# Six late token blocks take their first MLP product by Strassen's scheme

## The chip, the cores and the metric

The kernel runs on one core of a Trainium2 chip. The metric is the device time of one execution, in microseconds (us). A core has TensorE (PE, with PEld for its weight loads), VectorE (DVE), ScalarE (ACT), GpSimd (POOL) and SyncE (SP), which issues most transfers. TensorE writes its products into the eight banks of PSUM, and DVE and ACT take them from there.

## The reference

The input is 4 sequences of 3008 tokens with 256 features. A Fourier transform along the sequence, a complex 256x256 product with soft shrinkage, and the inverse transform give `x` again; then a two-layer MLP works on all 12032 tokens:

```python
X = np.fft.rfft(x, axis=1)
Yr = Xr @ w_r - Xi @ w_i + b_r;  Yi = Xr @ w_i + Xi @ w_r + b_i
Yr, Yi = shrink(Yr, 0.01), shrink(Yi, 0.01)
x = np.fft.irfft(Yr + 1j * Yi, n=3008, axis=1).reshape(12032, 256)
h = x @ w_in                          # 256 -> 2048
out = (h / (1 + exp(-h))) @ w_out     # 2048 -> 256
```

## The kernel before, in words

**Precision.** The large products run in the type fp32r on operands split into a high part and a low part, so one product is three matmuls: high by high, low by high and high by low. A "matmul" below is one instruction with a 128x128 weight; its cost goes with the columns that it streams.

**The MLP.** Tokens are taken in 24 blocks of 512 (the last, block 23, has 256). A block passes through 16 ticks, one for each 128 of the 2048 hidden features. In a tick `mlp1` makes six matmuls of 512 columns (L523: two halves of the 256 features, three terms each) into one PSUM bank `h`, of which there are two, and ACT writes Silu of it to `g` (L530). One tick later `split_g` makes the high part `gh` on ACT (L539) and the low part `gl` on DVE (L540). Two ticks after `mlp1`, `mlp2` multiplies them with `w_out` into four accumulator banks `acc`: for each 128 tokens one matmul of 512 columns (L562) and one of 256 (L566). After a block's last tick the four banks are added up and stored (`o`, ACT L582, DVE L583).

**The filler work.** The transforms of the four sequences are small steps that a table hangs on ticks, between a tick's `mlp1` and its `mlp2`: `at` puts a step on a tick, `put` on the next free one. `u3_step` (lines `s2_3`, `mix3`, `i1`) is one of twelve units of the middle transform of a sequence; for sequence 3 the units start at tick 190 and are 4.8 ticks apart. The last step, `i2`, multiplies stored rows with a table (L466) and splits the result into the high and the low part `xt` of a block's input (ACT L482, DVE L483); it comes in two halves and an end piece, `i2_ends` (L492 to L503, which hands leftover columns on to the next block as `rest`), each on a tick of its own, some 7, 5 and 3 ticks ahead of the block. Each engine works through its instructions in the order in which the program lists them, and waits on semaphores of the other engines.

The loop that lists the work of a tick:

```python
for t in range(len(ticks) + 2):
    split_g(*ticks[t - 1])
    ...
    mlp1(*ticks[t])
    for fn, args in fill.pop(t, []):
        fn(*args)
    flush(1 if t < 12 else 4)
    mlp2(*ticks[t - 2])
```

## Time and profile before

| | |
|---|---|
| runs | 1366.64, 1367.81, 1369.87 us; median 1367.81 |
| profiled execution | span 1366.0 us from first to last instruction; the page lists no time around it, and the median run is 1.8 us longer, the fastest 0.6 |
| PE | 1352.8 us busy, 99% |
| ACT, DVE | 727.9 us (53%), 686.1 us (50%) |
| chain that ended last | PE 96%, DMA 3%, ACT 1% |

The page gives each engine's busy time, then the span in slices, the transfers, the chain of work that ended last and the costliest groups. TensorE is busy for nearly the whole span, so the other views are read for what its instructions cost and for how closely ACT and DVE follow it.

### The profile page before, as it was taken

How to read it: one execution, taken by the hardware profiler on the slowest of the kernel's cores; microseconds unless marked ns; L12 is line 12 of the kernel's file. 1: busy time of each engine (PE TensorE's matmuls, PEld its weight loads, DVE VectorE, ACT ScalarE, POOL GpSimd, SP SyncE). 2: the span in 40 equal slices, each digit the busy share in tenths (PEclk: the TensorE clock that was granted, in tenths of full speed). 3: DMA queues.
4: the chain of work that ended last, by engine and by line, in shares of the span. 5: the costliest groups of instructions: out<-in, count | busy, mean ns of one | idle time of the engine just before them, and what ended most of it. 6: DMA issues, size and time to landing. Idle time of an engine off the chain costs nothing.

```text
span 1366.0 us, 20164 instructions
## 1 busy us (share of the span) xinstructions
PE 1352.8 (99%) x7589; PEld 1163.0 (85%) x7589; DVE 686.1 (50%) x1200; ACT 727.9 (53%) x1418; POOL 126.0 (9%) x192
## 2 busy tenths in 40 slices
...
GB/s 269 257 217 192 121 52 107 63 97 36 129 112 86 107 73 93 116 91 110 40 99 69 55 71 70 58 90 24 62 34 10 28 40 23 5 28 39 4 13 24
DMA packets 72753, 109.74 MB, mean 80 GB/s; under 512 B 8400, under 2 KB 54224, under 8 KB 72656
## 3 DMA queue, kind: packets, MB, share of 16 engines
...
q14 instruction: 37, 0.30, 0.1%
...
## 4 chain that ended last, share of the span: by engine, by line
PE 96%; DMA 3%; ACT 1%; issue 0%; DVE 0%; SPq 0%; ACTq 0%
PE h L523 38%; PE acc L562 25%; PE acc L566 13%; PE mix L376 6%; PE i L466 3%; PE s L351 2%; PE i L424 2%; PE mix L315 2%; PE s L254 1%; DMA scr<-i1o 1%; PE acc L557 1%; DMA scr<-s1o 1%; PE i2e L466 1%; PE i L421 1%; PE s L218 1%; PE s L294 1%
## 5 line engine op out<-in xcount | busy, mean ns | idle before, releaser
L523 PE MATMUL h<-xt,win 128*128 128x512 f32 (+1 forms) x2304 | 584.8, 389 | 0.0
L562 PE MATMUL acc<-wout,gh 128*128 128x512 f32 x1472 | 539.3, 400 | 0.0
L530 ACT ACTIVATE g<-h 128x512 f32<-128x512 f32 (+1 forms) x385 | 226.2, 588 | 511.2 <-PE h L523 509.2
L523 PEld LDWEIGHTS h<-xt,win 128*128 128x128 f32 x2304 | 400.9, 188 | 82.0 <-DVE xt L483 0.4
L540 DVE TENSOR_TENSOR gl<-g,gh 128x512 fp32r<-128x512 f32 (+1 forms) x385 | 264.6, 689 | 349.9 <-ACT gh L539 348.2
L566 PE MATMUL acc<-wout,gl 128*128 128x256 f32 x1472 | 411.9, 280 | 0.0
L562 PEld LDWEIGHTS acc<-wout,gh 128*128 128x128 f32 x1472 | 276.8, 188 | 58.6 <-issue 0.3
L566 PEld LDWEIGHTS acc<-wout,gl 128*128 128x128 f32 x1472 | 278.0, 189 | 9.7 <-issue 0.2
L539 ACT CAST gh<-g 128x512 fp32r<-128x512 f32 (+1 forms) x385 | 235.2, 611 | 5.2
L383 POOL TENSOR_TENSOR q<-q,bias 128x256 f32<-128x256 f32 x36 | 26.4, 734 | 592.8 <-ACT q L382 592.8
L483 DVE TENSOR_TENSOR xt<-i,xt 128x376 fp32r<-128x376 f32 (+2 forms) x48 | 28.1, 586 | 77.1 <-ACT xt L482 73.1
L256 DVE TENSOR_TENSOR s1o<-s,s1o 48x512 f32<-48x512 f32 x64 | 41.0, 678 | 48.2 <-ACT s1o L255 46.5
L466 PEld LDWEIGHTS i<-c_sb,gin 96*128 96x128 f32 x420 | 54.4, 192 | 9.6 <-issue 3.8
L396 DVE TENSOR_TENSOR y<-q,mix 64x256 f32<-64x256 f32 x144 | 60.3, 419 | 2.1
L466 PE MATMUL i<-c_sb,gin 96*128 96x94 f32 x420 | 53.7, 272 | 4.0 <-DMA gin<-scr 4.0
L245 DVE TENSOR_TENSOR sx<-x_sb,sx 47x1024 fp32r<-47x1024 f32 x32 | 40.7, 1271 | 22.3 <-ACT sx L244 21.4
L361 DVE TENSOR_TENSOR xs<-s,xs 128x256 f32<-128x256 f32 x36 | 15.3, 424 | 70.9 <-ACT xs L360 70.9
L184 POOL DMA_DIRECT2D x_sb<-in_x_dram x64 | 32.8, 514 | 142.4 <-ACT sx L244 125.4
L583 DVE TENSOR_TENSOR o<-acc,o 128x256 f32<-128x256 f32 x92 | 33.0, 417 | 24.4 <-ACT o L582 24.4
L351 PEld LDWEIGHTS s<-t,a 128*128 128x128 f32 x288 | 37.7, 191 | 3.0
L351 PE MATMUL s<-t,a 128*128 128x128 f32 x288 | 37.9, 274 | 0.0
L384 POOL TENSOR_TENSOR q<-q,bias 128x256 f32<-128x256 f32 x36 | 37.5, 1042 | 2.8
...
## 6 DMA issues: line engine op xcount, KB each, us to landing
...
```

The costliest lines, as they stand in the source:

```text
L245: nc.vector.tensor_sub(sx[64:64 + RR, :], t[64:64 + RR, :], sx[64:64 + RR, :])
L256: nc.vector.tensor_tensor(out=o[:, c], in0=p[:2 * NR, :], in1=o[:, c], op=ALU.add)
L351: nc.tensor.matmul(out=pv[:, e, :, r, :], lhsT=a[:, r, e * 128:(e + 1) * 128], rhs=t2[:, r * 128:(r + 1) * 128], start=True, stop=True,)
L376: nc.tensor.matmul(out=out, lhsT=x_[:, e, c, :], rhs=m[:, e, :], start=(n == 0), stop=(n == 5))
L396: nc.vector.tensor_tensor(out=y[64 * i:64 * i + 64, r, :], in0=q[rows, i, :], in1=pv[rows, i, :], op=op,)
L466: nc.tensor.matmul(out=p[:, o:o + m], lhsT=g_t[b, j // 4][:, q:q + 128], rhs=c4_sb[:, p0:p0 + m], start=True, stop=True,)
L523: nc.tensor.matmul(out=p[:, :n], lhsT=w[:, e, f * 128:(f + 1) * 128], rhs=v[:, e, :n], start=(m == 0), stop=(m == 5),)
L530: nc.scalar.activation(out=g[:, q], in_=p[:, q], func=ACTF.Silu)
L539: nc.scalar.copy(gh[:, q], g[:, q])
L540: nc.vector.tensor_sub(gl[:, q], g[:, q], gh[:, q])
L562: nc.tensor.matmul(out=a, lhsT=gh[:, q], rhs=wout[:, f].rearrange("p a c -> p (a c)"), start=begins, stop=False,)
L566: nc.tensor.matmul(out=a[:, D:2 * D], lhsT=gl[:, q], rhs=wout[:, f, 0, :], start=False, stop=ends,)
```

## The change

For blocks 17 to 22 the first product is made differently. Two ticks are taken together: their 256 hidden features by 512 tokens are a matrix product of 2x2 parts (two halves of the features in, of the hidden features and of the tokens), which Strassen's scheme, in Winograd's form, makes with seven products of parts instead of eight. Each is three matmuls of 256 columns, so a pair of ticks has 21 matmuls of 256 columns instead of 12 of 512.

Sums of parts of `w_in` are made once, on DVE and ACT, in eight steps after the last transform step (`fast_weights`). Sums of parts of a block's input (`fast_moving`) need the input in full precision, which `i2` now copies to `xf` on ACT as well (L491, L503, L513 of the changed kernel). In the even tick of a pair `fast_one` makes four products into both `h` banks, px and py; ACT copies the first to `u`, DVE adds the second to it (`u`) and the other two to that (`g[3]`). In the odd tick `fast_two` adds the other three products into the same banks, and Silu and the splitting follow there. `mlp2` of such a block comes three ticks after, not two. The six blocks' `i2` stands six ticks earlier than before, and the units of sequence 3 are 4.2 ticks apart, not 4.8. Buffers of the transforms move to a pool `tf`, which is released after the last transform step; the new buffers are then taken from its space (`tl`).

```diff
+FAST = range(17, 23)
...
     sb = ctx.enter_context(tc.tile_pool(name="sb", bufs=2))
+    tf = tc.alloc_tile_pool(name="tf", bufs=1)
...
         nc.scalar.copy(h[:, e, q], p[:, q])
         nc.vector.tensor_sub(l[:, e, q], p[:, q], h[:, e, q])
+        if i in FAST:
+            if e == 0:
+                xf[i] = tl.tile([128, 2, BLK], F32, tag="xf", bufs=1, name="xf")
+            nc.scalar.copy(xf[i][:, e, q], p[:, q])
...
             nc.scalar.copy(h[:, :, q], t)
             nc.vector.tensor_sub(l[:, :, q], t, h[:, :, q])
+            if i in FAST:
+                nc.scalar.copy(xf[i][:, :, q], t)
...
             nc.scalar.copy(h[:, :, q], p[:, :, 0:m])
             nc.vector.tensor_sub(l[:, :, q], p[:, :, 0:m], h[:, :, q])
+            if i in FAST:
+                nc.scalar.copy(xf[i][:, :, q], p[:, :, 0:m])
             rest[i + 1] = sb.tile([128, 2, NP], F32, tag="rest", bufs=1, name="rest")[:, :, 0:NP - m]
             nc.scalar.copy(rest[i + 1], p[:, :, m:NP])
...
+    HB = BLK // 2
+    xf, th, tw, fast = {}, {}, {}, {}
+    def fast_weights(q):
+        k = slice(q * 256, (q + 1) * 256)
+        f32 = tl.tile([128, 2, 256], F32, tag="td", bufs=1, name="wf")
+        d = tl.tile([128, 4, 128], F32, tag="wd", bufs=2, name="wd")
+        nc.vector.tensor_tensor(out=f32, in0=win[0][:, :, k], in1=win[1][:, :, k], op=ALU.add)
+        a11, a21 = f32[:, 0, 0:128], f32[:, 0, 128:256]
+        a12, a22 = f32[:, 1, 0:128], f32[:, 1, 128:256]
+        nc.vector.tensor_tensor(out=d[:, 0, :], in0=a21, in1=a22, op=ALU.add)
+        nc.vector.tensor_sub(d[:, 1, :], d[:, 0, :], a11)
+        nc.vector.tensor_sub(d[:, 2, :], a11, a21)
+        nc.vector.tensor_sub(d[:, 3, :], a12, d[:, 1, :])
+        yield
+        hi = tl.tile([128, 4, 128], F32R, name=f"sw_h{q}")
+        lo = tl.tile([128, 4, 128], F32R, name=f"sw_l{q}")
+        nc.scalar.copy(hi, d)
+        yield
+        nc.vector.tensor_sub(lo, d, hi)
+        tw[q] = (hi, lo)
+    def fast_moving(i):
+        x32 = xf.pop(i)
+        d = tl.tile([128, 4, HB], F32, tag="td", bufs=1, name="td")
+        l0, r0, l1, r1 = x32[:, 0, 0:HB], x32[:, 0, HB:BLK], x32[:, 1, 0:HB], x32[:, 1, HB:BLK]
+        nc.vector.tensor_sub(d[:, 0, :], r0, l0)
+        nc.vector.tensor_sub(d[:, 2, :], r1, r0)
+        nc.vector.tensor_sub(d[:, 1, :], r1, d[:, 0, :])
+        nc.vector.tensor_sub(d[:, 3, :], l1, d[:, 1, :])
+        yield
+        hi = tl.tile([128, 4, HB], F32R, tag="th", bufs=2, name="th")
+        lo = tl.tile([128, 4, HB], F32R, tag="tl", bufs=2, name="tl")
+        nc.scalar.copy(hi, d)
+        yield
+        nc.vector.tensor_sub(lo, d, hi)
+        th[i] = (hi, lo)
+    def fast_product(p, i, q, a, b, begins):
+        w = [v[:, a, :] for v in tw[q]] if isinstance(a, int) else \
+            [v[:, a[0], q * 256 + a[1] * 128:q * 256 + a[1] * 128 + 128] for v in win]
+        m = [v[:, b, :] for v in th[i]] if isinstance(b, int) else \
+            [v[:, b[0], b[1] * HB:(b[1] + 1) * HB] for v in xt[i]]
+        for n, (j, k) in enumerate(((0, 0), (1, 0), (0, 1))):
+            nc.tensor.matmul(
+                out=p, lhsT=w[j], rhs=m[k], start=(begins and n == 0), stop=(n == 2), skip_group_check=True,
+            )
+    def fast_one(i, q):
+        px, py = [ps.tile([128, 512], F32, tag="h", bufs=2, name="h") for _ in range(2)]
+        fast_product(px[:, 0:HB], i, q, (0, 0), (0, 0), True)
+        fast_product(px[:, HB:BLK], i, q, 0, 0, False)
+        fast_product(py[:, 0:HB], i, q, 1, 1, True)
+        fast_product(py[:, HB:BLK], i, q, 2, 2, False)
+        u = tl.tile([128, HB], F32, tag="u", bufs=2, name="u")
+        g = tl.tile([128, 4, HB], F32, tag="gp", bufs=2, name="gp")
+        nc.scalar.copy(u, px[:, 0:HB])
+        nc.vector.tensor_tensor(out=u, in0=py[:, 0:HB], in1=u, op=ALU.add)
+        nc.vector.tensor_tensor(out=g[:, 3, :], in0=px[:, HB:BLK], in1=u, op=ALU.add)
+        nc.vector.tensor_tensor(out=g[:, 3, :], in0=py[:, HB:BLK], in1=g[:, 3, :], op=ALU.add)
+        fast[i, q] = (px, py, u, g)
+    def fast_two(i, q):
+        px, py, u, g = fast.pop((i, q))
+        fast_product(px[:, 0:HB], i, q, (1, 0), (1, 0), False)
+        fast_product(px[:, HB:BLK], i, q, 3, (1, 1), False)
+        fast_product(py[:, HB:BLK], i, q, (1, 1), 3, False)
+        nc.scalar.activation(out=g[:, 0, :], in_=px[:, 0:HB], func=ACTF.Silu)
+        nc.vector.tensor_tensor(out=g[:, 1, :], in0=px[:, HB:BLK], in1=u, op=ALU.add)
+        nc.vector.tensor_tensor(out=g[:, 2, :], in0=py[:, HB:BLK], in1=u, op=ALU.add)
+        nc.scalar.activation(out=g[:, 1, :], in_=g[:, 1, :], func=ACTF.Silu)
+        gs = [tuple(tl.tile([128, 2, HB], F32R, tag=f"g{k}", bufs=4, name=f"g{k}") for k in "hl") for _ in range(2)]
+        def low(r):
+            nc.vector.tensor_sub(gs[r][1], g[:, 2 * r:2 * r + 2, :], gs[r][0])
+        nc.scalar.copy(gs[0][0], g[:, 0:2, :])
+        low(0)
+        nc.scalar.activation(out=g[:, 2:4, :], in_=g[:, 2:4, :], func=ACTF.Silu)
+        nc.scalar.copy(gs[1][0], g[:, 2:4, :])
+        later.append(lambda: low(1))
+        for r in range(2):
+            gf[i, 2 * q + r] = tuple(v.rearrange("p a c -> p (a c)") for v in gs[r])
+    later = []
...
-            t = 16 * i - 9 if i > 1 else -1
+            t = (16 * i - 15 if i in FAST else 16 * i - 9) if i > 1 else -1
             if i > 1:
                 at(t, i2_load, i)
             put(t + 2, i2, i, 0)
             put(t + 4, i2, i, 1)
-            put(t + 6, i2_ends, i)
+            t = put(t + 6, i2_ends, i)
+            if i in FAST:
+                moving = fast_moving(i)
+                for k in range(3):
+                    at(t + 2 + k, next, moving, None)
...
-        for b, t0, dt in ((1, t + 11, 3.1), (2, 104, 4.3), (3, 190, 4.8)):
+        for b, t0, dt in ((1, t + 11, 3.1), (2, 104, 4.3), (3, 190, 4.2)):
...
+        def swap_pools():
+            nonlocal tl
+            tf.release()
+            tl = ctx.enter_context(tc.tile_pool(name="tl", bufs=1, reuse_waits="tile"))
+        at(last + 1, swap_pools)
+        for q in range(NFF // 2):
+            steps = fast_weights(q)
+            for k in range(3):
+                at(last + 2 + q + k, next, steps, None)
+        assert last + 11 < 16 * FAST[0]
+        done = 0
         for t in range(len(ticks) + 2):
-            if 0 <= t - 1 < len(ticks):
+            i, f = ticks[t] if t < len(ticks) else (LAST, None)
+            if 0 <= t - 1 < len(ticks) and ticks[t - 1][0] not in FAST:
                 split_g(*ticks[t - 1])
             while deferred:
                 deferred.pop(0)()
-            if t < len(ticks):
-                mlp1(*ticks[t])
+            if i in FAST:
+                (fast_two if f % 2 else fast_one)(i, f // 2)
+            elif t < len(ticks):
+                mlp1(i, f)
+            if f is None or i not in FAST or f % 2 == 0:
+                while later:
+                    later.pop(0)()
             for fn, args in fill.pop(t, []):
                 fn(*args)
             flush(1 if t < 12 else 4)
-            if t >= 2:
-                mlp2(*ticks[t - 2])
+            while done < t - (2 if i in FAST else 1):
+                mlp2(*ticks[done])
+                done += 1
```

What the program lists for TensorE in such blocks: before, the end of one tick's `mlp2` and the next tick's `mlp1` (names as in the text, `win_80` and `win_81` are the high and the low part of `w_in`, `xt_9448` and `xt_9449` those of a block; in brackets the semaphores that an instruction waits for).

```order
L562 MATMUL acc<-wout,gh 128x512
L566 MATMUL acc<-wout,gl 128x256
L523 MATMUL h<-xt_9448,win_80 128x512 [waits Activation_49]
L523 MATMUL h<-xt_9448,win_81 128x512
L523 MATMUL h<-xt_9449,win_80 128x512
L523 MATMUL h<-xt_9448,win_80 128x512
L523 MATMUL h<-xt_9448,win_81 128x512
L523 MATMUL h<-xt_9449,win_80 128x512
```

After, the same place with `fast_two` (`sw`: sums of parts of `w_in`; `th`, `tl`: sums of parts of the input).

```order
L665 MATMUL acc<-wout,gh 128x512
L669 MATMUL acc<-wout,gl 128x256
L602 MATMUL h<-xt_10451,win_83 128x256 [waits DVE_49,Activation_49]
L602 MATMUL h<-xt_10451,win_84 128x256
L602 MATMUL h<-xt_10452,win_83 128x256
L602 MATMUL h<-xt_10451,sw_h_10375 128x256
L602 MATMUL h<-xt_10451,sw_l_10376 128x256
L602 MATMUL h<-xt_10452,sw_h_10375 128x256
L602 MATMUL h<-th,win_83 128x256 [waits DVE_49]
L602 MATMUL h<-th,win_84 128x256
L602 MATMUL h<-tl,win_83 128x256
```

The wait on ACT alone, for the release of a bank, became a wait on ACT and DVE: for the copy `u` and for the DVE addition L617 that reads the other half of px; the wait of the last three is for L618.

What it lists for ScalarE where a half of `i2` stands, before:

```order
L530 ACTIVATE g<-h 128x512 [waits DVE_49,PE_49]
L539 CAST gh<-g 128x512 [waits Activation_49]
L530 ACTIVATE g<-h 128x512 [waits DVE_49,PE_49]
L482 CAST xt_10879<-i_10881 128x376 [waits PE_49]
L539 CAST gh<-g 128x512 [waits Activation_49]
L530 ACTIVATE g<-h 128x512 [waits DVE_49,PE_49]
```

And after, from the Silu of `fast_two` to the next pair's:

```order
L627 ACTIVATE gp<-h 128x256 [waits PE_49]
L630 ACTIVATE gp<-gp 128x256 [waits DVE_49]
L636 CAST gh<-gp 128x512 [waits Activation_49]
L638 ACTIVATE gp<-gp 128x512 [waits DVE_49]
L639 CAST gh<-gp 128x512 [waits Activation_49]
L486 CAST xt_11408<-i_11410 128x376 [waits PE_49]
L491 COPY xf<-i_11410 128x376 [waits DVE_49]
L615 COPY u<-h 128x256 [waits PE_49]
L627 ACTIVATE gp<-h 128x256 [waits PE_49]
```

The copy `u` of the next pair now stands behind the whole splitting of this one and, where there is an `i2`, behind two copies of it, the second of which waits for DVE (its L487, which reads the same bank).

What it lists for VectorE at the end of a block, before:

```order
L540 TENSOR_TENSOR gl<-g,gh 128x512 [waits DVE_49,PE_49,Activation_49] x3
L583 TENSOR_TENSOR o<-acc,o 128x256 [waits DMAHW4_49,DMAHW3_49,Activation_49]
L583 TENSOR_TENSOR o<-acc,o 128x256 [waits DMAHW6_49,DMAHW7_49,DMAHW0_49,Activation_49]
L583 TENSOR_TENSOR o<-acc,o 128x256 [waits DMAHW2_49,DMAHW1_49,Activation_49]
L583 TENSOR_TENSOR o<-acc,o 128x256 [waits DMAHW4_49,DMAHW5_49,DMAHW3_49,Activation_49]
L540 TENSOR_TENSOR gl<-g,gh 128x512 [waits DVE_49,Activation_49]
```

And after:

```order
L616 TENSOR_TENSOR u<-h,u 128x256 [waits PE_49,Activation_49]
L617 TENSOR_TENSOR gp<-h,u 128x256 [waits DVE_49]
L618 TENSOR_TENSOR gp<-h,gp 128x256 [waits DVE_49]
L634 TENSOR_TENSOR gl<-gp,gh 128x512
L686 TENSOR_TENSOR o<-acc,o 128x256 [waits DMAHW1_49,DMAHW7_49,DMAHW0_49,Activation_49]
L686 TENSOR_TENSOR o<-acc,o 128x256 [waits DMAHW4_49,DMAHW3_49,Activation_49]
L686 TENSOR_TENSOR o<-acc,o 128x256 [waits DMAHW6_49,DMAHW5_49,Activation_49]
L686 TENSOR_TENSOR o<-acc,o 128x256 [waits DMAHW1_49,DMAHW7_49,DMAHW0_49,Activation_49]
L628 TENSOR_TENSOR gp<-h,u 128x256 [waits Activation_49]
L629 TENSOR_TENSOR gp<-h,u 128x256 [waits PE_49]
```

The four additions of the finished block's output, which stood between two `gl`, now stand between the two halves of a pair: ahead of L628 and L629, whose results the Silu of that pair needs. L628 waits for ACT too (its Silu L627, which reads the other half of px).

## Rows read from the trace of the kernel before

**Rows 1.** The page, part 1: engine, busy time, share of the span, instructions.

```profile
PE 1352.8 (99%) x7589; PEld 1163.0 (85%) x7589; DVE 686.1 (50%) x1200; ACT 727.9 (53%) x1418; POOL 126.0 (9%) x192
```

**Rows 2.** Busy time by stretch, a block: PE, PEld, DVE, ACT, POOL, granted clock, DMA.

```profile
1062.00:1109.00 47.00, 47.00 (x247) 39.96 (x246) 14.23 (x26) 21.84 (x42) 0.00 (x0) 1.00 0.08 20
```

**Rows 3.** The chain that ended last, 1290 to 1312 us: start, length, what.

```profile
1290.48 1.39 PE h L523 x6
...
1309.99 1.39 PE h L523 x6
```

**Rows 4.** The same chain, 470 to 490 us.

```profile
474.22 0.86 PE i L466 x8
...
481.56 0.42 PE i2e L466 x4
...
484.80 2.15 PE mix L376 x18
```

**Rows 5.** Groups of TensorE, 1000 to 1340 us: busy us, mean ns, idle before.

```profile
L566 PE MATMUL acc<-wout,gl 128*128 128x256 f32 x468 | 131.0, 280 | 0.0
```

**Rows 6.** Groups of ScalarE, 1000 to 1340 us.

```profile
L539 ACT CAST gh<-g 128x512 fp32r<-128x512 f32 x115 | 71.4, 621 | 2.7
...
L582 ACT COPY o<-acc 128x256 f32<-128x256 f32 x31 | 10.0, 376 | 0.0
L482 ACT CAST xt<-i 128x470 fp32r<-128x470 f32 x6 | 3.3, 553 | 2.9 <-PE i L466 2.9
L482 ACT CAST xt<-i 128x376 fp32r<-128x376 f32 x6 | 2.8, 474 | 1.6 <-PE i L466 1.6
L530 ACT ACTIVATE g<-h 128x256 f32<-128x256 f32 x2 | 0.8, 385 | 2.2 <-PE h L523 2.2
...
L500 ACT CAST xt<-i2e 128x112 fp32r<-128x112 f32 x1 | 0.3, 256 | 0.0
```

**Rows 7.** Groups of VectorE, 1000 to 1340 us.

```profile
L540 DVE TENSOR_TENSOR gl<-g,gh 128x512 fp32r<-128x512 f32 x115 | 79.6, 692 | 181.1 <-ACT gh L539 180.9
L583 DVE TENSOR_TENSOR o<-acc,o 128x256 f32<-128x256 f32 x30 | 10.7, 417 | 13.5 <-ACT o L582 13.5
L483 DVE TENSOR_TENSOR xt<-i,xt 128x470 fp32r<-128x470 f32 x6 | 3.9, 648 | 14.9 <-ACT xt L482 14.9
L483 DVE TENSOR_TENSOR xt<-i,xt 128x376 fp32r<-128x376 f32 x6 | 3.3, 550 | 13.1 <-ACT xt L482 13.1
...
L501 DVE TENSOR_TENSOR xt<-i2e,xt 128x112 fp32r<-128x112 f32 x1 | 0.3, 268 | 0.0
```

**Rows 8.** Groups of the whole span: two shapes that stand nearest to added ones.

```profile
L245 DVE TENSOR_TENSOR sx<-x_sb,sx 47x1024 fp32r<-47x1024 f32 x32 | 40.7, 1271 | 22.3 <-ACT sx L244 21.4
...
L362 ACT CAST xh<-xs 128x256 fp32r<-128x256 f32 x36 | 14.6, 407 | 17.8 <-DVE xs L361 17.8
```

**Rows 9.** Timeline of one tick: start, length, engine, instruction, idle and releaser.

```profile
1299.61 0.62 PE L523 MATMUL h<-xt,win 128*128 128x512 f32 x2
...
1300.27 0.60 ACT L530 ACTIVATE g<-h 128x512 f32<-128x512 f32 x1 [1.54 <-PE h L523]
...
1300.89 0.62 ACT L539 CAST gh<-g 128x512 fp32r<-128x512 f32 x1
...
1301.55 0.69 DVE L540 TENSOR_TENSOR gl<-g,gh 128x512 fp32r<-128x512 f32 x1 [2.09 <-ACT gh L539]
```

**Rows 10.** Timeline, 705 to 710 us: two ScalarE instructions in a row.

```profile
707.02 0.55 ACT L482 CAST xt<-i 128x470 fp32r<-128x470 f32 x1 [0.49 <-PE i L466]
...
707.47 0.62 ACT L539 CAST gh<-g 128x512 fp32r<-128x512 f32 x1
```

**Rows 11.** Timeline, 1293 to 1300 us: the output of a block on VectorE.

```profile
1295.59 1.42 DVE L583 TENSOR_TENSOR o<-acc,o 128x256 f32<-128x256 f32 x4 [1.71 <-ACT o L582]
```

**Rows 12.** Timeline, 36 to 37.5 us: matmuls after a wait, then without one.

```profile
36.14 0.48 PE L315 MATMUL mix<-wr,xh 128*128 128x256 f32 x2
...
36.58 0.40 PE L315 MATMUL mix<-wi,xh 128*128 128x256 f32 x2
```

**Rows 13.** Waits from 110 us on: who waited for whom, us, times, longest.

```profile
ACT rest L503 <- DVE xt L501: 8.8, 22, 0.9
```

More of the change, by code (lines that the diff above doesn't have):

```diff
@@ L206, in s1 @@
             tag, bufs = ("s1o", 2) if 8 * b + g in (6, 7, 10, 11) else ("gin", 4)
-            o = sb.tile([128, 4 * D], F32, tag=tag, bufs=bufs, name="s1o")[:96, :]
+            o = (tf if tag == "s1o" else sb).tile([128, 4 * D], F32, tag=tag, bufs=bufs, name="s1o")[:96, :]
         for i in range(2):
@@ L212, in s1 @@
                 k, w, n = ("x", 768, 2) if g % 2 else ("g", 512, 3)
-                hl = [sb.tile([128, w], F32R, tag=k + q, bufs=n, name="sx")[:, :512] for q in "hl"]
+                hl = [(tf if k == "x" else sb).tile([128, w], F32R, tag=k + q, bufs=n, name="sx")[:, :512] for q in "hl"]
                 nc.vector.tensor_copy(out=hl[0], in_=h)
@@ L229, in s1_later @@
         if i == 0:
-            x_t[1, g, "o"] = sb.tile([128, 4 * D], F32, tag="s1o", bufs=2, name="s1o")[:96, :]
+            x_t[1, g, "o"] = tf.tile([128, 4 * D], F32, tag="s1o", bufs=2, name="s1o")[:96, :]
         o = x_t[1, g, "o"]
@@ L242, in stack_split @@
         t = x_t[b, q]
-        sx = sb.tile([128, 4 * D], F32R, tag="sx", bufs=1, name="sx")
+        sx = tf.tile([128, 4 * D], F32R, tag="sx", bufs=1, name="sx")
         nc.scalar.copy(sx[:64 + RR, :], t[:64 + RR, :])
@@ L249, in stack_product @@
         sx = x_t.pop((b, q))
-        o = sb.tile([128, 4 * D], F32, tag="s1o", bufs=2, name="s1o")[:2 * NR, :]
+        o = tf.tile([128, 4 * D], F32, tag="s1o", bufs=2, name="s1o")[:2 * NR, :]
         for i in range(2):
@@ L276, in t2_load @@
     def t2_load(b, u):
-        t2 = sb.tile([128, 256], F32, tag="t2", bufs=3, name="t2")
+        t2 = tf.tile([128, 256], F32, tag="t2", bufs=3, name="t2")
         nc.sync.dma_start(out=t2, in_=c2[:, u * 256:(u + 1) * 256])
@@ L283, in u_load @@
             t2_load(b, u)
-        a = sb.tile([128, 2, D], F32, tag="a", bufs=3, name="a")
+        a = tf.tile([128, 2, D], F32, tag="a", bufs=3, name="a")
         nc.sync.dma_start(out=a, in_=scr1[b][2 * u:2 * u + 2].rearrange("r p d -> p r d"))
@@ L297, in s2 @@
                 )
[L298 to L299 removed]
+        xh = tf.tile([128, 4, 192], F32R, tag="xh", bufs=2, name="xh")
+        xl = tf.tile([128, 4, 192], F32R, tag="xl", bufs=2, name="xl")
         nc.scalar.copy(xh[:, :, 64:192], pv)
@@ L329, in mix3_weights @@
     def mix3_weights():
-        t = sb.tile([128, 2, 2 * D], F32, tag="s1o", bufs=2, name="w32")
+        t = tf.tile([128, 2, 2 * D], F32, tag="s1o", bufs=2, name="w32")
         nc.sync.dma_start(out=t[:, :, 0:D], in_=w_r.rearrange("(e p) d -> p e d", p=128))
@@ L379, in mix3 @@
         p = bank("mix")
-        q = sb.tile([128, 2, D], F32, tag="q", bufs=1, name="q")
+        q = tf.tile([128, 2, D], F32, tag="q", bufs=1, name="q")
         product(p[:, 0:D], 2, wr)
@@ L406, in split_z @@
         y = u_t[b, u]
-        zh = sb.tile([128, 2, D], F32R, tag="zh", bufs=2, name="zh")
-        zl = sb.tile([128, 2, D], F32R, tag="zl", bufs=2, name="zl")
+        zh = tf.tile([128, 2, D], F32R, tag="zh", bufs=2, name="zh")
+        zl = tf.tile([128, 2, D], F32R, tag="zl", bufs=2, name="zl")
         nc.scalar.copy(zh, y)
```

50 lines of the change are left out of this document (25 added, 25 removed).

## The prediction

> **What bounds the kernel now.** I read the page's engine line first, then busy time by stretch, the chain, the groups by shape, and the timeline of one tick. PE is busy for 1352.8 of 1366.0 us [rows 1]. In the stretch of a block it is busy for all of 47.00 us at a granted clock of 1.00 (of 2.4 GHz), while DVE works 14.23 and ACT 21.84 us [rows 2]. The chain consists of `mlp1` and `mlp2` without a gap: seven ticks take 1309.99 - 1290.48 = 19.51 us, 2.787 each, of which six matmuls of L523 are 1.39 [rows 3] and `mlp2` the other 1.40. So here every us taken from PE is worth one, as long as nobody keeps PE waiting. ACT follows an end of PE after 0.04 us, and DVE and ACT follow each other after some 0.03 [rows 9]; today nobody waits for them, as two `h` banks give each bank a whole tick of slack.
>
> **What PE saves.** A matmul of 512 columns costs 1.39 / 6 = 0.232 us [rows 3]; one of 256 in a row without waits 2.15 / 18 = 0.119 [rows 4]. A pair goes from 12 x 0.232 = 2.78 to 21 x 0.119 = 2.51 us of products, with two `mlp2` of 1.40 from 5.58 to 5.31. Six blocks are 48 pairs: **-13.0 us**. (An eighth of 2.78 would be 0.35 a pair; the narrow ones cost 0.119, not half of 0.232, and give 0.08 of it back.)
>
> **The new loop.** Both `h` banks now belong to one pair, so the next pair can't start on them while this one is read, and its halves depend on each other. Follow a pair from the start S of `fast_two`:
> - six matmuls into px: 5 x 0.119 + 0.28 (one matmul from start to end [rows 5]) + 0.04 = 0.92
> - Silu of px on ACT, 256 columns, 0.385 [rows 6] + 0.03
> - `g[1]` on DVE (L628 waits for that Silu, which reads the same bank), 0.417 like an output addition [rows 7] + 0.03
> - Silu of `g[1]`, from SBUF, at 0.41 like a copy of that size [rows 8] + 0.03
> - high part of the first tick, 0.62 [rows 6], less 0.10, by which two independent ACT instructions overlap (707.02 + 0.55 against 707.47 [rows 10])
> - Silu and high part of the second tick: 0.62 + 0.03, then 0.62 - 0.10
> - copy `u` of the next pair, 0.376 [rows 6] + 0.03; addition `u`, 0.417 + 0.03; `g[3]`, 0.417 + 0.05, for which the next `fast_two` waits (L617 reads px).
>
> Sum 5.23 us against 5.31 of PE. The loop fits with 0.08 to spare: in a pair where ACT and DVE do nothing else PE doesn't wait, and where anything stands in between it does. An earlier `u` copy doesn't help, as it stands behind the splitting on ACT. What stands in between, per block (of ACT and DVE the `i2` of the block after next to start, `fast_moving`, and the output of the block before):
>
> 1. Pair with the block end and the first half of `i2`. On DVE L618, L634 and four additions (1.42 [rows 11]) follow `g[3]`: -0.05 + 0.45 + 0.69 + 1.42 less three overlaps of 0.083 ((4 x 0.417 - 1.42) / 3) end 2.26 after S, and L628 would have started at 1.34: 0.92 late. `i2` puts cast, DVE subtraction and the new copy `xf` ahead of `u`; the copy waits for the subtraction, as today `rest` waits (22 times [rows 13]). For 470 columns 0.553 + 0.03 + 0.648 + 0.03 + 0.553 - 0.10 = 1.71, for 376 0.474, 0.550 and 0.474 give 1.46 [rows 6, 7]; mean 1.59. PE has 0.86 more for eight matmuls, 1.08 for ten [rows 4]; mean 0.97. Loop 5.23 + 0.92 + 1.59 = 7.74, PE 6.28: wait **1.46**.
> 2. Second half of `i2`: 6.82 against 6.28: **0.54**.
> 3. `i2_ends`: two casts and three copies of about 0.26, three overlaps, a wait of 0.30 for DVE [rows 6, 7]: 1.30. 6.53 against 5.31 + 0.42 [rows 4]: **0.80**.
> 4. First step of `fast_moving`: on DVE, after the high part of the first tick, `gl` 0.72 and four subtractions of 256 columns, 2.29 with overlaps and handoffs, where ACT needs 1.58 to the end of `u`: 0.71 late. **0.63**.
> 5. Its third step, one subtraction of 1024 elements, 1.27 [rows 8]: 0.33 late. **0.25**.
>
> That is 3.68 us, and five restarts of 0.08 (a first matmul after a wait 0.48, else 0.40 [rows 12]): 4.08 per block. Blocks 17 to 21 have all five: **+20.4**. Block 22 has no later `i2` to make, only the block end: 0.92 - 0.08 + 0.08 = **+0.9**.
>
> **Once each.** Entry into block 17: `fast_two` follows `fast_one` with no `mlp2` between, since these come a tick later. L616 waits for all 12 matmuls (1.43 + 0.16 + 0.04), then 0.45 and 0.47: `g[3]` is there 2.55 after the start, PE at 1.43: **+1.1**. The weight sums put on DVE, for eight ticks, one addition of 512 and one subtraction of 512 elements and four of 128 beside `gl`: 3 x 0.69 + 4 x 0.28 less overlaps = 2.96 us a tick, where a tick has 2.79; what piles up, 8 x 0.17 = **1.4**, comes back as a wait of `mlp2` for `gl`. From zero, if it runs off beside later ticks, to 3.0, if the block end there meets the backlog whole; I take 1.4, as no fewer DVE instructions are listed.
>
> **At nothing.** Units of sequence 3 at 4.2 ticks: those of sequence 2 stand at 4.3 and PE waited for none. `i2` six ticks earlier keeps its two ticks from load to use. New buffers in the released space wait for transfers that ended many ticks before. On the exit from block 22 `mlp2` goes back to two ticks, with banks free. If a cover of these fails, it is one wait of 1 to 2 us.
>
> Sum: -13.0 + 20.4 + 0.9 + 1.1 + 1.4 = +10.8. The span goes from 1366.0 to 1376.8, the median, 1.8 above it before, to **1378.6**.
>
> **Bounds.** PE's part is bounded by 0.119 and by L523's half, 0.116 (another -3.0). The loop has ten handoffs: at 0.02 to 0.05 us each it is 5.1 to 5.45. At 5.1 the five waits lose 0.13 each, -3.3 in all; at 5.45 they gain 0.22 each and the other pairs wait 0.14 and a restart: +11. If casts after a wait overlap more, or `xf` and `u` are cheaper from PSUM, each loaded pair loses up to 0.3: -8. So the likeliest's own range is 1370 to 1390.
>
> **Rivals.**
> A. *Waits don't bind, faster.* If the waits were by halves of a bank, `fast_two` would start after `u` alone, and `g[1]` would not wait for Silu: the loop loses 0.47 + 0.42 and is 4.34, and the longest loaded pair comes to 6.85 against 6.28. Then -13.0 + 5 x 0.65 + 1.4 gives 1359.5; with no wait at all 1354.8. For it: ACT and DVE work 14 and 22 of 47 us [rows 2], half idle. Against it: `rest` waits for `xt` of other columns of its bank today [rows 13], and the listed waits of L602 and L628 name both engines. It decides once the loaded loops are under 6.28. 0.15.
>
> The Trainium skill ("PSUM — Partial Sum Buffer", "PSUM bank collisions raise a hardware error") has PSUM guarded by bank and quadrant of partitions, not by address, with the two readers ACT and DVE included; the trace agrees, with 8.8 us of ACT waiting in that place [rows 13]. It speaks against this change, whose halves of one bank are read by both.
>
> B. *No change.* Loaded loops cost half, because the bursts fall into the slack of neighbouring pairs: -13.0 + 10.2 + 3.4 = +0.6, 1368.4. Against it: a loop's slack is 0.08 a pair, and only pairs 6 to 8 of a block could return a delay, which on PE can't be returned. 0.08.
>
> C. *Every pair waits.* Handoffs that are 0.02 longer than taken make the loop 5.43: each of 48 pairs waits 0.12 and 0.08: +9.6, 1388. For it: a margin of 0.08 over ten steps. 0.09.
>
> D. *Weight loads show.* PEld is busy 39.96 / 246 = 0.162 us per load [rows 2]; with a matmul of 0.119 that can't hide: 21 x 0.162 - 2.78 = +0.62 a pair, +30: about 1398, as the longer PE time covers most waits. Against it: the 18 matmuls of `mix`, 0.119 each with loads between [rows 4]. 0.02.
>
> The Trainium skill ("TensorE: Matmul & The Clock Gate", "Back-to-back issue gap") puts narrow matmuls beside loads at a higher price per column too: about 81 ns sustained for 128 columns, 131 ns for 512. An estimate between these, 98 ns for 256, would make a pair 21 x 0.098 - 12 x 0.131 = 0.49 us longer, the kernel 23 us; the rows (232 and 119 ns [rows 3, 4]) disagree with both figures, so the rule has no more than D's chance.
>
> **Chances and range.** The forecast 0.66. A measurement of this kernel can't tell 0.2% (1365.1 to 1370.5) from no change. Faster: A, 0.15. Within: B and a low end of the forecast, 0.09. Slower: 0.76. The range runs from 1364, which leaves most of A out, to 1391, which leaves D and the tail of C out.
>
> **What would show it.** In the changed profile: 21 matmuls of L602 in 2.51 us without waits; PE idle by some 20 to 25 us in all, mostly before `fast_two` and named after DVE L617, at intervals of eight pairs; ACT's chain Silu, cast, `u` unbroken there; blocks 17 to 21 of about 47.0 - 8 x 0.27 + 4.08 = 48.9 us, block 22 near 44.6 - 2.16 + 0.9 = 43.3. Rival A shows as PE busy throughout and blocks of some 45, C as a wait in each pair, D as spacings of 0.16 with PEld full. If PE's idle time lies elsewhere than in these five pairs, my loop is wrong even where the sum is right.

## The result and the profile after

The changed kernel takes 1382.91 us (median; 1382.30 to 1384.66) against 1368.38 of the kernel before in the same comparison: a ratio of 1.0109, 95% interval 1.0095 to 1.0124, so 14.5 us slower. The forecast was 1378.6, 10.8 slower. The profiled execution has a span of 1381.3 us, 15.3 more than before.

The page's engine line (engine, busy time, share of the span, instructions) stands against [rows 1]:

```profile
PE 1350.9 (98%) x8021; PEld 1175.2 (85%) x8021; DVE 809.9 (59%) x1518; ACT 767.9 (56%) x1552; POOL 125.9 (9%) x192
```

PE works 1.9 us less in a span that is 15.3 longer: its idle time went from 13.2 to 30.4. (That the product's saving shows as 1.9 only is taken up in the last section.) DVE gained 124 us of work and ACT 40. Busy time by stretch, for block 18, from its first product to that of block 19 (the columns as in [rows 2]):

```profile
1109.01:1158.54 49.53, 46.36 (x318) 41.82 (x317) 31.88 (x70) 27.88 (x62) 0.00 (x0) 1.00 0.07 20
```

PE, busy for all of 47.00 us in [rows 2], is now busy for 46.36 of block 18's 49.53 us, at the same clock; before, that block took 46.80. TensorE's waits from 1000 us on (who waited for whom: us in total, times, longest):

```profile
PE h L602 <- DVE gp L617: 16.6, 27, 1.2
PE acc L665 <- DVE o L686: 1.1, 1, 1.1
```

L602 is the matmul of all seven products, `gp` the program's name for `g`, and L617 DVE's addition to `g[3]`, the last one to read px. All 27 waits of L602 are at a start of `fast_two`: one at the entry, five in each of blocks 17 to 21, one in block 22. TensorE's timeline of block 18 (start, length, instruction, idle time before it and its releaser):

```profile
1122.12 0.59 PE L602 MATMUL h<-xt,win 128*128 128x256 f32 x3 [1.23 <-DVE gp L617]
1129.03 0.59 PE L602 MATMUL h<-xt,win 128*128 128x256 f32 x3 [0.49 <-DVE gp L617]
1135.83 0.59 PE L602 MATMUL h<-xt,win 128*128 128x256 f32 x3 [0.81 <-DVE gp L617]
1141.90 0.59 PE L602 MATMUL h<-xt,win 128*128 128x256 f32 x3 [0.48 <-DVE gp L617]
1147.64 0.59 PE L602 MATMUL h<-xt,win 128*128 128x256 f32 x3 [0.16 <-DVE gp L617]
```

Five waits, in the five pairs that the forecast named, and then three pairs with none listed. But those three take 5.45 us, where PE's own work was put at 5.31 (and is 5.34 to 5.35, as the experiments below show). The timelines of ACT, DVE and PE over one such pair show why:

```profile
1103.56 0.59 PE L602 MATMUL h<-xt,win 128*128 128x256 f32 x3
...
1104.54 0.38 ACT L627 ACTIVATE gp<-h 128x256 f32<-128x256 f32 x1 [2.05 <-PE h L602]
1104.96 0.42 DVE L628 TENSOR_TENSOR gp<-h,u 128x256 f32<-128x256 f32 x1 [0.49 <-ACT gp L627]
1105.42 0.42 ACT L630 ACTIVATE gp<-gp 128x256 f32<-128x256 f32 x1 [0.49 <-DVE gp L628]
1105.87 0.62 ACT L636 CAST gh<-gp 128x512 fp32r<-128x512 f32 x1
1106.39 0.63 ACT L638 ACTIVATE gp<-gp 128x512 f32<-128x512 f32 x1
1107.06 0.62 ACT L639 CAST gh<-gp 128x512 fp32r<-128x512 f32 x1
1107.58 0.36 ACT L615 COPY u<-h 128x256 f32<-128x256 f32 x1
...
1107.98 0.42 DVE L616 TENSOR_TENSOR u<-h,u 128x256 f32<-128x256 f32 x1 [0.77 <-ACT u L615]
1108.44 0.42 DVE L617 TENSOR_TENSOR gp<-h,u 128x256 f32<-128x256 f32 x1
1109.01 0.59 PE L602 MATMUL h<-xt,win 128*128 128x256 f32 x3
```

(Rows of the three engines are put in order of time.) From L627 on each row starts 0.03 to 0.04 us after the row above it ends, or overlaps it on ACT, and PE follows L617 after 0.15: this is the loop of the forecast, unbroken, and it is 5.45 us long, where 5.23 was worked out. PE's wait here is so short that the view lists none; it shows only as 0.59 for the first three matmuls, which take 0.53 where nothing is waited for.

Where a block's end and an `i2` come together, in the pair that starts at 1114.46 (ACT and DVE):

```profile
1115.29 1.41 DVE L686 TENSOR_TENSOR o<-acc,o 128x256 f32<-128x256 f32 x4
1116.62 0.41 DVE L628 TENSOR_TENSOR gp<-h,u 128x256 f32<-128x256 f32 x1
...
1118.04 0.63 ACT L638 ACTIVATE gp<-gp 128x512 f32<-128x512 f32 x1
...
1119.22 0.47 ACT L486 CAST xt<-i 128x376 fp32r<-128x376 f32 x1
1119.72 0.55 DVE L487 TENSOR_TENSOR xt<-i,xt 128x376 fp32r<-128x376 f32 x1 [0.86 <-ACT xt L486]
1120.31 0.47 ACT L491 COPY xf<-i 128x376 f32<-128x376 f32 x1 [0.62 <-DVE xt L487]
1120.68 0.38 ACT L615 COPY u<-h 128x256 f32<-128x256 f32 x1
```

L628 starts 2.16 us after the pair's start (forecast 2.26), and `u` is issued 1.46 after L486, as worked out.

### The profile page after: what moved, and what is told of

It reads as the page before. It is cut to its first block, busy times and chain, and to the rows that moved or that the text cites. A ratio compares the mean times of both kernels' runs of the same rounds, so it can differ in the third digit from the quotient of the medians.

```text
span 1381.3 us, 21395 instructions
## 1 busy us (share of the span) xinstructions
PE 1350.9 (98%) x8021; PEld 1175.2 (85%) x8021; DVE 809.9 (59%) x1518; ACT 767.9 (56%) x1552; POOL 125.9 (9%) x192
## 4 chain that ended last, share of the span: by engine, by line
PE 82%; ACT 7%; DVE 6%; DMA 3%; issue 2%; DVEq 0%; SPq 0%; ACTq 0%
PE h L535 28%; PE acc L665 21%; PE acc L669 10%; PE mix L380 6%; PE h L602 5%; PE i L470 3%; PE s L355 2%; PE i L428 2%; PE mix L319 2%; ACT gh L636 1%; PE s L258 1%; DVE gp L617 1%; DVE u L616 1%; ACT gp L630 1%; DVE gp L628 1%
## 5 line engine op out<-in xcount | busy, mean ns | idle before, releaser
L535 PE MATMUL h<-xt,win 128*128 128x512 f32 (+1 forms) x1728 | 436.4, 388 | 0.0
L542 ACT ACTIVATE g<-h 128x512 f32<-128x512 f32 (+1 forms) x289 | 168.7, 584 | 362.3 <-PE h L535 360.4
L535 PEld LDWEIGHTS h<-xt,win 128*128 128x128 f32 x1728 | 299.8, 188 | 61.0 <-DVE xt L487 0.4
L552 DVE TENSOR_TENSOR gl<-g,gh 128x512 fp32r<-128x512 f32 (+1 forms) x289 | 198.1, 688 | 183.5 <-ACT gh L551 180.7
L551 ACT CAST gh<-g 128x512 fp32r<-128x512 f32 (+1 forms) x289 | 175.7, 608 | 2.8
L634 DVE TENSOR_TENSOR gl<-gp,gh 128x512 fp32r<-128x512 f32 x96 | 65.9, 687 | 39.3 <-ACT gh L636 38.8
L387 POOL TENSOR_TENSOR q<-q,bias 128x256 f32<-128x256 f32 x36 | 26.4, 734 | 570.0 <-ACT q L386 570.0
L602 PE MATMUL h<-xt,win 128*128 128x256 f32 x288 | 53.5, 294 | 16.7 <-DVE gp L617 16.6
L602 PEld LDWEIGHTS h<-xt,win 128*128 128x128 f32 x288 | 40.4, 188 | 30.2 <-issue 26.9
L627 ACT ACTIVATE gp<-h 128x256 f32<-128x256 f32 x48 | 18.4, 384 | 84.7 <-PE h L602 84.7
L487 DVE TENSOR_TENSOR xt<-i,xt 128x376 fp32r<-128x376 f32 (+2 forms) x48 | 28.1, 586 | 61.5 <-ACT xt L486 57.6
L365 DVE TENSOR_TENSOR xs<-s,xs 128x256 f32<-128x256 f32 x36 | 15.3, 424 | 71.9 <-ACT xs L364 71.9
```

The source lines that it names most:

```text
L535: nc.tensor.matmul(out=p[:, :n], lhsT=w[:, e, f * 128:(f + 1) * 128], rhs=v[:, e, :n], start=(m == 0), stop=(m == 5),)
L542: nc.scalar.activation(out=g[:, q], in_=p[:, q], func=ACTF.Silu)
L551: nc.scalar.copy(gh[:, q], g[:, q])
L552: nc.vector.tensor_sub(gl[:, q], g[:, q], gh[:, q])
L602: nc.tensor.matmul(out=p, lhsT=w[j], rhs=m[k], start=(begins and n == 0), stop=(n == 2), skip_group_check=True,)
L634: nc.vector.tensor_sub(gs[r][1], g[:, 2 * r:2 * r + 2, :], gs[r][0])
```

## The experiments

Ten runs. Each table row gives what a kernel needs for the pairs of block 18, from one start of `fast_two` to the next (pair 1 has the block end and the first half of `i2`, pair 2 the second half, pair 3 `i2_ends`, pairs 4 and 5 the first and the third step of `fast_moving`; plain pairs have nothing of the kind), and in the last two columns the time from the Silu of tick 0 to that of tick 271, the last before block 17, and from there to the Silu of the last tick (the first of its two):

| kernel | pair 1 | 2 | 3 | 4 | 5 | plain | to tick 271 | from there |
|---|---|---|---|---|---|---|---|---|
| before | | | | | | | 945.98 | 305.52 |
| forecast for after | 7.69 | 6.77 | 6.61 | 6.02 | 5.64 | 5.31 | | |
| after | 7.66 | 6.91 | 6.80 | 6.07 | 5.74 | 5.45 | 947.37 | 319.46 |
| e1_u_first | 6.87 | 6.28 | 6.10 | 6.06 | 5.74 | 5.35 to 5.41 | 948.22 | 306.36 |
| e2_i2_even | 6.53 | 6.21 | 5.94 | 6.72 | 5.73 | 5.46 | 947.42 | 309.33 |
| e3_old_product | | | | | | | 947.61 | 305.51 |
| e4_narrow_alone | | | | | | | 948.71 | 294.08 |
| e5_gl_late | 7.06 | 6.91 | 6.78 | 6.06 | 5.74 | 5.45 | 948.70 | 315.80 |
| e6_xf_sum | 6.76 | 6.29 | 6.34 | 6.11 | 5.73 | 5.45 | 948.54 | 309.84 |
| e7_best | 6.21 | 6.21 | 5.76 | 5.34 | 5.39 | 5.35 | 953.09 | 295.96 |
| e8_order_only | 6.22 | 6.20 | 5.76 | 5.99 | 5.73 | 5.34 to 5.41 | 948.28 | 301.04 |
| e9_spread | 6.22 | 6.21 | 5.75 | 5.34 | 5.38 | 5.35 | 946.80 | 295.92 |
| e10_u_twice | 8.05 | 7.85 | 7.12 | 6.06 | 5.86 | 5.86 | 947.45 | 335.69 |

Up to tick 271 kernels that list the same differ by up to 1.3 us (after and e5_gl_late), so smaller differences in that column, or in a median, say nothing.

**e3_old_product: everything but the product.**

```diff
+PAIRS = ()
...
-            if i in FAST:
+            if i in PAIRS:
                 (fast_two if f % 2 else fast_one)(i, f // 2)
```

> Everything of the change (pools, order of the steps, sums of w_in, xf copies, fast_moving) with the old product in blocks 17 to 22, so the sums are made and not used. My theory: only the sums of w_in cost PE time, 1.4 us, before block 17; the blocks keep their 47.0 and 44.6 us: about 1369.8. Rival: the added copies and subtractions delay also the old product, by the 3 us per block that PE waited in the changed kernel: about 1383.

Measured: 1368.88 us, ratio 1.0010 (0.9997 to 1.0023). From tick 271 on it is 305.51 against 305.52: the copies `xf`, the steps of `fast_moving` and the earlier `i2` cost nothing beside the old product. To tick 271 it is 1.6 longer, with the one PE wait of 1.1 us for `o` in it. So from block 17 on the added work is free beside the old product; it costs only in the new loop.

**e4_narrow_alone: the narrow matmuls without the loop** (with `PAIRS = ()` as in e3).

```diff
+        if i in FAST:
+            fast_halves(p, i, f)
+        for e in range(0 if i in FAST else 2):
...
+        part = all[10:] if f % 2 else all[:10]
+        for n, (w, m) in enumerate(part):
+            nc.tensor.matmul(
+                out=p[:, 0:HB] if n < 5 else p[:, HB:BLK], lhsT=w, rhs=m, ...
```

> As the kernel with the old product, but a tick's mlp1 in blocks 17 to 22 makes 10 or 11 of the seven products' 21 matmuls of 256 columns, into one bank with Silu of 512 columns as before; no u, no additions between the banks. It leaves out the combination, so what it computes in these blocks is not the product. My theory: PE's own gain is 13.0 us and nobody waits: 1369.8 - 13.0 = 1356.8. Rival: narrow matmuls between wide ones cost more, and the 5.45 us of an undisturbed pair are PE's: -13.0 + 48 x 0.14, about 1363.5.

Measured: 1357.07 us, ratio 0.9921 (0.9904 to 0.9939). The product in the chain of waits (start, length, what), an odd and an even tick:

```profile
1104.13 1.31 PE h L558 x11
...
1106.86 1.20 PE h L558 x10
```

1.31 + 1.20 = 2.51 us, as forecast. But between them lie 1106.86 - 1104.13 - 1.31 = 1.42 us of `mlp2`, where it took 1.40; block 18 is 44.88 us against 46.80 in e3, 0.24 a pair and not 0.27, and the whole stretch 305.51 - 294.08 = 11.4 us shorter, not 13.0. Why `mlp2` is 0.02 longer there stays open.

**e1_u_first: the copy `u` ahead of the second tick's high part.**

```diff
-        nc.scalar.copy(gs[1][0], g[:, 2:4, :])
-        later.append(lambda: low(1))
+        later.append(lambda: (nc.scalar.copy(gs[1][0], g[:, 2:4, :]), low(1)))
```

> The high part of a pair's second tick (L639) and its low part are listed after the next pair's copy u instead of ahead of it; nothing else changes. My theory: the pair's loop goes through ACT's order, so every loop that ends in u gets 0.52 us shorter. Pairs without other work fall from 5.45 us to PE's own 5.31; the three pairs with i2 work from 7.66, 6.91 and 6.80 to 7.14, 6.39 and 6.28; the two pairs of fast_moving stay at 6.07 and 5.74, since DVE sets them. Per block -2.0, in all -11: about 1372. Rival 1: the 0.14 us of the pairs without other work is a price of PE itself at a restart; they stay at 5.45 and the sum is -8.3, about 1374.6. Rival 2: DVE sets all waits; nothing changes, 1383.

Measured: 1368.76 us, ratio 1.0003 (0.9991 to 1.0014): one instruction's place gives back 14 us. Plain pairs fall to 5.35 (one of the three to 5.41), which disproves rival 1, the two pairs that DVE sets stay at 6.06 and 5.74, and the others lose more than expected. The gain per loop is 0.65, not 0.52: L639 also waits 0.03 for its Silu, and with it gone the cast of `xt` overlaps that Silu. From L638 to L486 it was 1119.22 - 1118.04 = 1.18, and is 0.53 in ACT's timeline (the other 0.14 that pair 1 lost is on DVE: L628 starts 2.03 us after the pair's start, not 2.16):

```profile
1114.53 0.63 ACT L638 ACTIVATE gp<-gp 128x512 f32<-128x512 f32 x1
1115.06 0.46 ACT L486 CAST xt<-i 128x376 fp32r<-128x376 f32 x1
```

**e10_u_twice: the loop made longer.**

```diff
         nc.scalar.copy(u, px[:, 0:HB])
+        nc.scalar.copy(u, px[:, 0:HB])
```

> The changed kernel with the copy u made twice in a row (the second writes the same values); nothing else. My theory: the loop is what an undisturbed pair takes, so 0.27 us more on ACT (0.37 less the overlap of 0.10) come out in full: 5.45 to 5.72, and the three pairs with i2 by as much; the two pairs of fast_moving, set by DVE, stay at 6.07 and 5.74. 6 pairs of five blocks and some 5 of block 22: +9.5, about 1392.5. Rival: an undisturbed pair is PE's own, and only the pairs that waited before get longer: 3 x 0.27 x 5 = +4, about 1387.

Measured: 1399.38 us, ratio 1.0227 (1.0202 to 1.0253). In ACT's timeline the second copy, which writes the same tile again, doesn't overlap the first, and costs 0.40, not 0.27:

```profile
1104.58 0.37 ACT L615 COPY u<-h 128x256 f32<-128x256 f32 x1
1104.98 0.38 ACT L616 COPY u<-h 128x256 f32<-128x256 f32 x1
```

A plain pair went from 5.45 to 5.86, by the full 0.40, and PE's wait is now long enough to be listed:

```profile
1106.42 0.60 PE L602 MATMUL h<-xt,win 128*128 128x256 f32 x3 [0.28 <-DVE gp L618]
```

With e1 this brackets the loop: 0.65 taken off ends at PE's floor, 0.40 put on comes out whole. Pair 4 didn't move, since DVE sets it; pair 5 rose to the loop's 5.86. Pair 2 of block 18 rose by 0.94, of which some 0.5 isn't the loop's but TensorE's clock (the columns as in [rows 2]):

```profile
1127.80:1131.30 3.50, 3.50 (x16) 3.11 (x15) 1.79 (x4) 2.57 (x6) 0.00 (x0) 0.52 0.00 0
```

PE had waited 1.61 us before that pair; then the granted clock was 0.52, nearly all of it at the lower of the two levels (1.2 of 2.4 GHz). Block 21 shows the same. In blocks 17, 19 and 20, after the same wait, the clock stayed at 1.00 and pair 2 rose by 0.40.

**e5_gl_late: one DVE instruction behind the next two.**

```diff
         nc.vector.tensor_tensor(out=g[:, 2, :], in0=py[:, HB:BLK], in1=u, op=ALU.add)
+        while later:
+            later.pop(0)()
...
-            if f is None or i not in FAST or f % 2 == 0:
+            if f is None or i not in FAST:
```

> The changed kernel with one DVE instruction moved: the low part of a pair's second tick (the later L634) is listed behind L628 and L629 of the next pair, not ahead of them. My theory: of the 0.9 us by which the block end delays L628, 0.6 are this instruction; the pair with the block end falls from 7.66 to about 7.05 in blocks 17 to 21 and from 6.19 to about 5.58 in block 22, and all other pairs keep 5.45 to 6.91, since there L634 ends before L628 is due. In all -3.7: about 1379.2. Rival: the four output additions cost by holding the accumulators or by their DMAs, and where L634 stands makes no difference: 1382.9.

Measured: 1378.41 us, ratio 1.0096 (1.0075 to 1.0118). The pair with the block end fell to 7.06, in block 22 from 6.19 to 5.60, all others stayed; from tick 271 on 3.7 us shorter, as expected to the tenth. The block end acts through the order on DVE.

**e6_xf_sum: no copies `xf` on ACT.**

```diff
-            nc.scalar.copy(xf[i][:, e, q], p[:, q])
...
-        x32 = xf.pop(i)
+        x32 = tl.tile([128, 2, BLK], F32, tag="xf", bufs=1, name="xf")
+        nc.gpsimd.tensor_tensor(out=x32, in0=xt[i][0], in1=xt[i][1], op=ALU.add)
...
+        yield
...
-                for k in range(3):
-                    at(t + 2 + k, next, moving, None)
+                for k in (0, 2, 3, 4):
+                    at(t + k, next, moving, None)
```

> The changed kernel without the copies xf on ACT: the input in full precision is made by one addition on POOL, of the high and the low part that lie in SBUF; the rest stays where it was. My theory: the copies, and their wait for DVE, are 1.1 us of the loop in a half of i2 and some 0.6 in i2_ends. Pair with block end and first half 7.66 to about 6.6, second half 6.91 to PE's 6.2, i2_ends 6.80 to about 6.2; a block -2.3, in all -11.5: about 1371.4. Rival: the casts xt alone are enough to hold u up, as they wait for PE's i2 which comes after the mlp1; then less than 3 us in all, about 1380.

Measured: 1372.71 us, ratio 1.0046 (1.0031 to 1.0061). Pairs 1 to 3 fell to 6.76, 6.29 and 6.34; from tick 271 on 9.6 us shorter. The copies were most of what `i2` put into the loop. What is left of it on ACT ahead of `u` are the casts `xt`, and in pair 3 also the copy `rest`, which waits 0.41 us for DVE; pairs 2 and 3 stay 0.1 and 0.6 above PE's 6.21 and 5.76.

**e2_i2_even: `i2` on the other ticks.**

```diff
-            t = (16 * i - 15 if i in FAST else 16 * i - 9) if i > 1 else -1
+            t = (16 * i - 14 if i in FAST else 16 * i - 9) if i > 1 else -1
...
-                    at(t + 2 + k, next, moving, None)
+                    at(t + 1 + k, next, moving, None)
```

> The steps of i2 for the six blocks stand on even ticks (with fast_one, so that on ACT they come behind u) instead of odd ones; the steps of fast_moving stay where they were. My theory: the xt and xf copies in front of u were the wait; the pairs with i2 work then take what PE takes, 6.28, 6.28 and about 6.0, and the pair with the block end alone 6.19, as block 22 has it. A block goes from 49.5 to about 46.9; five blocks -13: about 1370. Rival: the copies only move to another place of the same loop (ahead of Silu of px), and the three pairs keep their waits of 1.23, 0.49 and 0.79: 1383.

Measured: 1373.23 us, ratio 1.0040 (1.0023 to 1.0058). Pairs 1 to 3 fell to 18.7 us together, as expected, but pair 4 rose to 6.72. ACT's timeline there shows the rival at work in one place:

```profile
1132.77 0.31 ACT L510 CAST xt<-i2e 128x176 fp32r<-128x176 f32 x1
1134.95 0.31 ACT L513 COPY xf<-i2e 128x176 f32<-128x176 f32 x1 [1.88 <-DVE xt L511]
1135.16 0.17 ACT L515 COPY rest<-i2e 128x12 f32<-128x12 f32 x1
1135.22 0.40 ACT L627 ACTIVATE gp<-h 128x256 f32<-128x256 f32 x1
```

L511 stands on DVE behind the pair's additions and L634, and ACT waits 1.88 us for it in order; Silu of px, due 0.98 after the pair's start at 1133.59, is 0.65 late. The move gained 2.0 a block and not 2.6.

**e8_order_only and e7_best: the moves together, without and with POOL.** e8_order_only is e1, e5 and e2 at once. e7_best also has the sum `xf` and these on POOL:

```diff
-        nc.vector.tensor_sub(d[:, 0, :], r0, l0)
+        nc.gpsimd.tensor_sub(d[:, 0, :], r0, l0)
...
-        nc.vector.tensor_sub(lo, d, hi)
+        nc.gpsimd.tensor_sub(lo, d, hi)
...
-                    at(t + 2 + k, next, moving, None)
+                for k in (1, 4, 5):
+                    at(t + k, next, moving, None)
```

> The first three of those moves only (u ahead, low part late, i2 on even ticks); nothing on POOL, so the copies xf and the DVE steps of fast_moving and of the sums stay. My theory: the waits that remain are the entry (1.1), the backlog of the sums (1.2) and the two steps of fast_moving, 0.5 and 0.15 us with a restart each, per block; a block takes 45.8 us or little more where i2_ends meets the first step: about 1364. Rival: the gain of the kernel with everything comes from POOL, and this one stays near the 1368.8 of the kernel with u ahead.

> All moves together: u ahead of the second tick's high part, its low part behind g[1] and g[2], i2 on even ticks, xf as a sum on POOL, the subtractions of fast_moving on POOL at wider steps, the low part of the sums of w_in on POOL. My theory: every loop is then below PE's time, PE waits only at the entry into block 17 (1.1 us), and a block takes 8 x 5.34 plus its i2, about 45: 1368.4 - 11.3 (the product, by the blocks of the kernel with narrow matmuls alone) + 1.1 + 0.3 = 1358.5. Rival: POOL and DVE slow each other down in SBUF, additions on DVE get longer and the loop binds again: 1363 to 1368.

Measured: 1365.16 us, ratio 0.9981 (0.9968 to 0.9994), and 1363.98 us, 0.9981 (0.9966 to 0.9995). e8_order_only is 1 us from what was expected, e7_best 5.5 above it. From tick 271 on they take 301.04 and 295.96 us; in e7_best every pair is at PE's time. But before that e7_best took 5.7 us more than the changed kernel. Its waits of PE, and DVE and POOL in the sums of `w_in`:

```profile
PE acc L660 <- DVE o L681: 3.4, 1, 3.4
PE h L595 <- DVE gp L610: 1.1, 1, 1.1
```

```profile
1004.30 1.62 POOL L567 TENSOR_TENSOR sw_l<-wd,sw_h 128x512 fp32r<-128x512 f32 x1 [1.28 <-ACT sw_h L565]
```

```profile
1004.88 1.20 DVE L558 TENSOR_TENSOR wd<-wf 128x128 f32<-128x128 f32 x1
1006.11 0.29 DVE L559 TENSOR_TENSOR wd<-wd,wf 128x128 f32<-128x128 f32 x1
```

In seven of the eight sums one of DVE's operations on 128 columns takes 1.18 to 1.26 us beside a subtraction on POOL, and not 0.29: moving 0.68 us from DVE to POOL put 0.9 back on DVE, and the wait for `o` grew from 1.1 to 3.4. Behind it came a second price (the columns as in [rows 2]):

```profile
1016.90:1020.00 3.10, 3.10 (x9) 2.66 (x10) 2.76 (x5) 0.78 (x2) 1.28 (x1) 0.51 0.25 62
```

After 3.4 us without work TensorE ran 3.1 us at a granted clock of 0.51, nearly all of it at 1.2 of 2.4 GHz, and at 1.00 again from 1020 us on; the changed kernel kept 1.00 behind its wait of 1.1. Half the clock for 3.1 us is some 1.5 us (an estimate), so wait and clock are 3.8 of the 5.7; the rest is little more than that column varies by. The rival was right in that place. In the blocks, too, L629 (`gl`) took 1.10 us in the mean beside POOL and 0.69 alone, but there nobody waits for it: every pair keeps PE's time.

**e9_spread: e7_best with the sums back on DVE, at a wider spacing** (the diff shows the spacing).

```diff
-                at(last + 2 + q + k, next, steps, None)
+                at(last + 2 + q * 3 // 2 + k, next, steps, None)
```

> As the kernel with all moves together, but the low part of the sums of w_in is back on DVE and the eight sums start one and a half ticks apart instead of one. My theory: the 3.4 us that PE waited before block 17 in that kernel came from DVE waiting for POOL with the output additions behind it; at this spacing DVE has 2.3 us of work in a tick of 2.8, nothing piles up, and both that wait and the 1.1 us of the changed kernel are gone. From block 17 on it stays at -9.6 against before: about 1368.3 - 9.6 + 0.3 = 1359. Rival: the wait belongs to the block end, whatever stands on DVE, and 1.1 us or more remain: 1360.5 to 1362.

Measured: 1358.52 us, ratio 0.9934 (0.9915 to 0.9952), the fastest of all. TensorE's only wait after the transforms, and a block (PE, PEld, DVE, ACT, POOL, clock, DMA):

```profile
PE h L595 <- DVE gp L610: 1.1, 1, 1.1
```

```profile
1098.48:1143.42 44.94, 44.94 (x319) 41.99 (x317) 30.38 (x65) 26.70 (x59) 8.46 (x6) 1.00 0.07 22
```

The wait for the output is gone. Up to that place this kernel differs from e8_order_only, which waits 1.1 us there, in the spacing alone, so the backlog came from the spacing. A block is PE's again, with most of Strassen's gain: from tick 271 on 9.6 of 11.4 us, and 1.1 of what is missing is the entry wait. In all it is 9.5 us below the kernel before (1367.97 in this comparison).

## Why the prediction was right, and where it was off

The forecast's direction and its cause hold: the product saves PE time, and a loop through ACT and DVE takes back more. Rival A is out (27 waits, and L628 never starts before L627, which reads the same bank, has ended: 0.03 us behind it in 42 of the 48 pairs, 0.78 in the six with a block end); so is B, as no later pair returned a delay; D too, with 2.51 us for 21 matmuls. Step by step:

- **The product, -13.0:** measured -11.4 (e3 against e4). The 21 matmuls take the 2.51 us that were worked out from [rows 4]; the missing 0.03 a pair is in `mlp2` beside them.
- **The loop, 5.23:** this is the term that was mis-sized; it is 5.45. Silu of px starts 0.98 after S, not 0.92, as the first matmul after a wait is late by 0.06; and from L617 to the next `fast_two` it is 0.57, not 0.47. The rest, eight handoffs and instructions on ACT and DVE, comes to 3.90 against 3.84. The restart was known from [rows 12], but I added it only to the five loaded pairs, although a loop contains it in each turn. So I had 0.08 of slack where there was none, and called plain pairs PE's; rival C, at 5.43, had the better loop, and what came is a mixture: C's 0.1 in plain pairs, with the five waits besides.
- **Durations** that were taken from other instructions of [rows 6 to 8] hold. Groups of ScalarE in the changed kernel, 1050 to 1320 us (busy us, mean ns, idle before), for which 0.41, 0.385 and 0.376 were assumed:

```profile
L630 ACT ACTIVATE gp<-gp 128x256 f32<-128x256 f32 x42 | 17.5, 418 | 25.1 <-DVE gp L628 25.1
L627 ACT ACTIVATE gp<-h 128x256 f32<-128x256 f32 x42 | 16.1, 384 | 72.2 <-PE h L602 72.2
L615 ACT COPY u<-h 128x256 f32<-128x256 f32 x43 | 16.0, 372 | 0.9 <-PE h L602 0.9
```

- **Five loaded pairs, +20.4:** over blocks 17 to 21 they take 7.76, 7.02, 6.66, 6.07 and 5.74 in the mean against a forecast of 7.82, 6.90, 6.61, 6.02 and 5.64; with the plain pairs a block is 49.6, not 48.9. Against e9's, whose pairs are at PE's time (45.2), the loops cost 4.4 a block: +22.0, to which block 22 adds 1.5 (forecast 0.9). That pair 1 came so close is luck: its loop was 0.14 longer than forecast even with the restart, and L628 0.76 late (2.16 after the start, against 1.40 in a plain pair) where 0.92 was forecast.
- **Parts of these:** the block end through L634 (e5: 0.60 expected and measured), the copies `xf` (e6), `u` behind L639 (e1), each moved its own pairs and no others.
- **Entry, +1.1:** L602 waited 1.12 at 1059.49. **Sums of `w_in`, +1.4:** the size holds, +1.4 to tick 271, as far as a column that varies by 1.3 can show it. The wait is another: not of `mlp2` for `gl`, but 1.1 us at its start, for accumulators that L686 has still to read, behind the sums on DVE; it is gone in e9.
- **At nothing:** held (e3; the exit from block 22, which e3 doesn't have, lists no wait).

So -11.4 + 22.0 + 1.5 + 1.1 + 1.4 = +14.6, against 15.3 in the two profiles. The remaining 0.7 lies behind tick 271 (13.9 longer there, where the terms give 13.2), and most of it is in e9 too: its blocks 17 to 21 take 225.97 us together and e4's 225.40. Why, stays open.
